# A fused Fourier transform and MLP: relayouts that read two slots twice, and a new order of the opening

## The chip, the cores and the metric

The kernel runs on one core of one Trainium2 chip. The core has a matrix engine (PE; its weight loads are PEld), a vector engine (DVE), an activation engine (ACT), a general engine (POOL), and SP, which here only issues transfers. Transfers can be issued from SP, ACT and POOL, each with a queue of its own; they share 16 DMA engines. The metric is the device time of one execution in microseconds, lower is better.

## The reference

For an input `x` of 8 batches x 3136 rows x 256 columns, what must be computed is

```python
X = np.fft.fft(x, axis=1)
X = np.fft.fft(X, axis=2)
x = X.real
mu, var = x.mean(-1), x.var(-1)
xn = (x - mu) / np.sqrt(var + 1e-06) * g_ln
out = x + np.maximum(xn @ w_ch1, 0.0) @ w_ch2
```

with `w_ch1` of 256 x 1024 and `w_ch2` of 1024 x 256. Both weights arrive as float64, and the kernel takes them apart on the chip.

## The kernel before, in words

**Two steps of the long transform.** 3136 = 64 x 49. Step 1 makes length-64 transforms: for each batch, seven pairs of slots, folded on DVE or POOL (`fold_zw`, `fold_eo`), multiplied on PE (`step1`, L272 to L280), copied from PSUM by ACT (L284), and stored by `store1` (L288) to a scratch in DRAM. The scratch holds 16 slots of 128 x 256 floats. Step 1 fills 14; the other two are cleared once for each of the two scratches by `clear_scratch` (L236), from zeros in the tile `warm`.

**The relayout.** `relayout` (L291, transfer on L295) reads the scratch back into a tile `s2` with another meaning of the 128 rows: row = slot * 8 + r, with 16 groups of 256 floats in each row. The source steps through 16 slots of 8 rows, 128 rows at one distance; each row is a run of up to 4096 floats. Batch 0 is read in four pieces (groups 0 to 2, 2 to 4, 4 to 8, 8 to 16: 256, 256, 512 and 1024 KB). Batches 1 to 7 are read in one transfer of 2048 KB each.

**Step 2 and the MLP.** `step2` (L328) multiplies `s2` by a table `tab_s`, a group at a time; it uses the first 112 rows (14 slots) as K. L332 adds the zero frequency, once a batch, in the first `step2` of that batch. ACT casts the result to `ckh` (L349) and copies it to `ck` (L351), and DVE makes the rest `ckl` (L353). Then the tokens run in chunks of 256, in 8 steps of a chunk each: `moe1_a` (L373: w1 in a high and a low part, 6 matmuls; ACT copies to `asb`, L378; DVE makes `h`, L379 and L380), `moe1_b` (ACT makes `h_hi`, L387; DVE `h_lo`, L388) and `moe2` (L423: w2 in two parts, 12 matmuls). `residual` and its helpers (L448 and on) do the row transform and the statistics, `finish` (L493 and on) the result, and `store_out` (L504) the stores of 256 KB.

**The weights.** Both float64 weights come in four quarters. `convert_z` on ACT (L550) takes the exponent, `convert_m` on DVE (L541, L543) the mantissa, `convert_b` on DVE (L555 a maximum, L556 a shift) mends the exponent, and `finish_w1` or `finish_w2` (L584, L616) multiplies. `transform_w1` (L594), `round_w1` (L602), `rest_w1` (L607) and `rest_w1_copy` (L612) fold a transform into w1; they need the tile `minus` (L775). `split_w2` makes w2's two parts on ACT (L560) and POOL (L561). The w2 quarters are loaded by `load_w2` (L575) into the tiles that held the w1 quarters, so each waits for w1's conversions from that tile.

**What sets the order.** PE, ACT, DVE and POOL run in an order written out by hand. The start is the long list of calls in the function's last part, in which SP keeps the written order too. Afterwards a loop over the steps of all chunks calls `moe1_b`, `moe1_a`, what a table `late` has for that step, `moe2` of three steps before, and what a table `after` has. Relayouts of batches 1 to 7 stand in `after`, 2 steps behind the batch's last store.

## Time and profile before

| What | Value |
|---|---|
| Median of 3 runs | 989.21 us (988.85 to 989.91) |
| The profiled execution | 989.4 us, of which the span is 987.6 us |
| PE busy | 975.3 us, 99% of the span |
| DVE, ACT, POOL busy | 813.1, 535.3, 249.8 us |
| Granted TensorE clock | 1.00 |
| Moved by DMA | 94.94 MB, 96 GB/s in the mean |
| A whole relayout, issue to landing | 7.9 us median, 7 of them |

Busy time is that in which an engine executes something. A row of the timeline gives the start and the length in us, then the engine, line and operation with its output and inputs, and in brackets the idle time before it with what ended that. "Issue to landing" of a transfer goes from the instruction that issues it to the last byte's arrival. Windows cut the span in stretches and list each engine's busy time within. A line of the waits has the engine and line that waits, what it waited for, the sum in us, how often, and the longest.

### The profile page before, as it was taken

The page shows a single profiled execution, that of the slowest core. Times are in us where ns is not written, and L with a number is a line of the kernel's source. Part 1 is how long each engine was busy: PE and PEld are TensorE (multiplying, and loading weights), DVE is VectorE, ACT ScalarE, POOL GpSimd, SP SyncE. Part 2 cuts the span into 40 slices and gives each one's busy share as a digit, 9 for nine tenths or more (in the row PEclk, how much of TensorE's full clock was granted, in tenths as well). Part 3 has the DMA queues.
Part 4 walks back from the last instruction along what each step waited for, and adds up shares of the span by engine and source line. Part 5 has one row for each costly group of instructions (what it writes and reads, how often), then busy time and mean ns, then how long its engine had stood idle before and what let it go on. Part 6 is the DMA issues. An engine that isn't in the chain of part 4 may idle for free.

```text
span 987.6 us, 22017 instructions
## 1 busy us (share of the span) xinstructions
PE 975.3 (99%) x8410; PEld 961.6 (97%) x8411; DVE 813.1 (82%) x2194; ACT 535.3 (54%) x1416; POOL 249.8 (25%) x279
## 2 busy tenths in 40 slices
PE   9899999999999999999999999999999999999998
PEld 5689999999999999999999999999999999999998
DVE  6788887888888888878888888888888888888887
ACT  3656555555555555555555556555555554555553
POOL 2147343224322332322342234223322300000000
PEclk9999999999999999999999999999999999999999
DMA  9923352214221242112421232212311112100101
GB/s 350 377 80 130 101 188 76 87 54 158 79 96 55 76 168 90 65 65 71 176 86 55 86 150 87 97 55 73 121 52 37 54 50 102 44 23 22 44 23 44
DMA packets 42297, 94.94 MB, mean 96 GB/s; under 512 B 4240, under 2 KB 19088, under 8 KB 41168
## 3 DMA queue, kind: packets, MB, share of 16 engines
q1 hardware_dynamic: 40016, 90.19, 25.4%
q10 hardware_dynamic: 1776, 2.04, 0.6%
q8 instruction: 67, 1.10, 0.5%
q0 software_dynamic: 400, 1.31, 0.3%
q14 instruction: 38, 0.31, 0.1%
HBM read 52.62 MB, written 40.89 MB: 95 GB/s over the span
## 4 chain that ended last, share of the span: by engine, by line
PE 94%; DVE 3%; DMA 1%; ACT 1%; issue 0%; ACTq 0%; SPq 0%; DVEq 0%
PE acc L423 52%; PE ab L373 26%; PE ps L328 6%; PE psy L448 5%; PE ps L280 3%; DVE h_lo L388 1%; DMA scratch<-s 1%; PE pw L701 1%; PE ps L272 0%; DMA s<-scratch 0%; PE ps L274 0%; DVE h L379 0%; DVE h L380 0%; ACT h_hi L387 0%; PE bb L373 0%
## 5 line engine op out<-in xcount | busy, mean ns | idle before, releaser
L423 PE MATMUL acc<-w_hi,h_lo 128*128 128x256 f32 x1568 | 434.1, 277 | 1.2 <-ACT w_hi L560 0.9
L423 PE MATMUL acc<-w_lo,h_hi 128*128 128x256 f32 x1568 | 433.8, 277 | 1.0 <-POOL w_lo L561 1.0
L423 PE MATMUL acc<-w_hi,h_hi 128*128 128x256 f32 x1568 | 433.6, 277 | 0.0
L388 DVE SCALAR_TENSOR_TENSOR h_lo<-h,h_hi 128x512 fp32r<-128x512 f32 x392 | 294.7, 752 | 141.8 <-ACT h_hi L387 139.3
L387 ACT ACTIVATE h_hi<-h 128x512 fp32r<-128x512 f32 x392 | 250.1, 638 | 292.2 <-DVE h L380 292.1
L423 PEld LDWEIGHTS acc<-w_hi,h_lo 128*128 128x128 f32 x1568 | 294.6, 188 | 1.9 <-ACT w_hi L560 1.1
L423 PEld LDWEIGHTS acc<-w_lo,h_hi 128*128 128x128 f32 x1568 | 294.4, 188 | 1.2 <-POOL w_lo L561 1.2
L423 PEld LDWEIGHTS acc<-w_hi,h_hi 128*128 128x128 f32 x1568 | 294.5, 188 | 0.0
L373 PE MATMUL ab<-ckl,w_hi 128*128 128x256 f32 x768 | 218.1, 284 | 2.2 <-DVE h L380 2.1
L373 PE MATMUL ab<-ckh,w_lo 128*128 128x256 f32 x768 | 212.8, 277 | 0.3 <-ACT ckh L349 0.3
L373 PE MATMUL ab<-ckh,w_hi 128*128 128x256 f32 x768 | 212.5, 277 | 0.0
L231 POOL TENSOR_TENSOR fl<-f,fh 128x512 fp32r<-128x512 f32 x49 | 64.0, 1306 | 504.6 <-ACT fh L225 472.5
L379 DVE TENSOR_TENSOR h<-asb,ab 128x256 f32<-128x256 f32 x384 | 158.6, 413 | 1.3 <-ACT asb L378 1.3
L380 DVE TENSOR_TENSOR h<-asb,ab 128x256 f32<-128x256 f32 x384 | 158.7, 413 | 0.0
L373 PEld LDWEIGHTS ab<-ckl,w_hi 128*128 128x128 f32 x768 | 144.3, 188 | 3.4 <-issue 3.4
L373 PEld LDWEIGHTS ab<-ckh,w_lo 128*128 128x128 f32 x768 | 144.4, 188 | 0.5 <-ACT ckh L349 0.5
L373 PEld LDWEIGHTS ab<-ckh,w_hi 128*128 128x128 f32 x768 | 144.3, 188 | 0.0
L378 ACT COPY asb<-ab 128x256 f32<-128x256 f32 x384 | 137.8, 359 | 8.9 <-PE ab L373 1.3
L284 ACT COPY s<-ps 128x508 f32<-128x508 f32 x56 | 32.8, 585 | 62.6 <-PE ps L280 51.2
L328 PE MATMUL ps<-tab_s,s 112*128 112x98 f32 (+1 forms) x512 | 65.6, 273 | 1.0 <-DMA s<-scratch 1.0
L328 PEld LDWEIGHTS ps<-tab_s,s 112*128 112x128 f32 x512 | 61.8, 192 | 1.5 <-issue 1.5
L349 ACT CAST ckh<-ps 128x392 fp32r<-128x392 f32 (+49 forms) x112 | 39.7, 356 | 41.8 <-PE ps L328 41.5
(113 smaller groups left out, 969.1 us busy)
## 6 DMA issues: line engine op xcount, KB each, us to landing
xs<-x SPq DMA_DIRECT2D x56, 512.0 KB, 4.4
out<-o SPq DMA_DIRECT2D x96, 256.0 KB, 2.0
s<-scratch SPq DMA_DIRECT2D x7, 2048.0 KB, 7.9
scratch<-s SPq DMA_DIRECT2D x49, 256.0 KB, 2.4
w1p_all<-w SPq DMA_DIRECT2D x6, 512.0 KB, 8.9
scratch<-s POOLq DMA_DIRECT2D x4, 256.0 KB, 6.6
w1p_all<-w ACTq DMA_DIRECT2D x2, 512.0 KB, 5.6
s<-scratch SPq DMA_DIRECT2D x1, 1024.0 KB, 10.8
```

Of the source, the lines that this page charges most:

```text
L231: nc.gpsimd.tensor_tensor(out=lo, in0=f, in1=hi.bitcast(F32), op=ALU.subtract)
L284: nc.scalar.copy(s[:, :, :, :127], ps[:, :, :, :127])
L328: nc.tensor.matmul(ps[:, h, k0 - base:k1 - base], s2[b][:KP, g, 128 * h:128 * h + 128], tab_s[:KP, h, k0:k1], start=(h == 0 and g == 2 * j ...
L349: nc.scalar.copy(hi, src)
L373: nc.tensor.matmul(pt, wt[wi][:, j, fs], ch[xi][:, j, :w], start=(n == 0), stop=(n == 2))
L378: nc.scalar.copy(asb[:, :w], pa)
L379: nc.vector.tensor_tensor(out=h[:, :w], in0=asb[:, :w], in1=pb, op=ALU.add)
L380: nc.vector.tensor_tensor(out=h[:, w:], in0=asb[:, :m], in1=pb[:, :m], op=ALU.subtract)
L387: nc.scalar.activation(h_hi, h, AF.Relu)
L388: nc.vector.scalar_tensor_tensor(out=h_lo, in0=h, scalar=0.0, in1=h_hi.bitcast(F32), op0=ALU.max, op1=ALU.subtract)
L423: nc.tensor.matmul(acc[c, i][:, side], hs[xi][:, h0:h0 + 128], ws[wi][:, f], start=(f == 0 and side == 0 and n == 0), stop=(f == 7 and n = ...
L448: nc.tensor.matmul(ps[:, j, :n], ck[:, j], ty_s[:, j, :n], start=(j == 0), stop=True, skip_group_check=True)
```

## The change

Five things change.

1. The scratch has 14 slots, and nothing is cleared. A relayout reads 16 slots all the same: eight from slot 0 on and eight from slot 6 on, so slots 6 and 7 are read twice. The source of the transfer is written as 2 groups at a distance of 6 slots, 8 slots in each, and the rows of a slot; the 8 slots and their 8 rows are at one distance and make 64 rows. The destination stays 128 rows. The second copy of slots 6 and 7 falls on rows 64 to 79 of `s2`. The table has zeros there, and `step2` multiplies over all 128 rows.
2. The first piece of `tab` is issued by ACT, behind the last store of batch 0 and the load of w2's first quarter, and no longer by SP ahead of them. The first quarter of w2 is loaded ahead of ACT's conversion of w1's third quarter; the second quarter is loaded by SP between two pieces of the relayout, and no longer by ACT; the third comes behind the third piece.
3. The maximum (`convert_x`, from `convert_b`) moves from DVE to POOL for w1's last two quarters and all four of w2.
4. Conversions, splits and copies of the opening stand at other places: w2's second quarter ahead of the first cast to `ckh`, the split of `t1` near it, the copies to `ck` later, w2's last quarter earlier.
5. The first chunk's second `residual_e` comes one step later.

**SP around the relayout of batch 0.** `s_0` is the tile `s2`, `w1p_all` the tile in which the quarters of w2 arrive. Before:

```order
L570 DMA w1p_all<-w 128x512 x2
L760 DMA tab_s<-tab 128x2x393
L761 DMA tz_s<-tz 128x50
L295 DMA s_0_259<-scratch_93 128x512 x2
L575 DMA w1p_all<-w 128x2x256
L295 DMA s_0_259<-scratch_93 128x1024
L773 DMA tab_s<-tab 128x2x392
L295 DMA s_0_259<-scratch_93 128x2048
L575 DMA w1p_all<-w 128x2x256
```

Changed:

```order
L574 DMA w1p_all<-w 128x512 x2
L763 DMA tz_s<-tz 128x50
L292 DMA s_0_262<-scratch_93 128x1x512 x2
L579 DMA w1p_all<-w 128x2x256
L292 DMA s_0_262<-scratch_93 128x1x1024
L579 DMA w1p_all<-w 128x2x256
L777 DMA tab_s<-tab 128x2x392
L292 DMA s_0_262<-scratch_93 128x1x2048
L579 DMA w1p_all<-w 128x2x256
```

The piece of `tab` ahead of `tz` is gone, a load of w2 stands between the two small pieces and the third, another behind the third, and the destination of a relayout has a dimension of 1 in it.

**ACT behind the last store of batch 0.** `ew_2` and `ew_3` are exponents of w1's last two quarters. Before:

```order
L288 DMA scratch_93<-s_0_134 128x2x256
L550 ACTIVATE ew_2_245<-w1p_all 128x512
L575 DMA w1p_all<-w 128x2x256
L550 ACTIVATE ew_3_252<-w1p_all 128x512
L575 DMA w1p_all<-w 128x2x256
L775 CAST minus<-tw_all 128x128
```

Changed:

```order
L283 DMA scratch_93<-s_0_134 128x2x256
L579 DMA w1p_all<-w 128x2x256
L550 ACTIVATE ew_2_244<-w1p_all 128x512
L550 ACTIVATE ew_3_251<-w1p_all 128x512
L768 DMA tab_s<-tab 128x2x393
L779 CAST minus<-tw_all 128x128
```

ACT issues one load of w2 in place of two, ahead of both conversions, then the piece of `tab`, and `minus` stands behind that.

**ACT around the first casts of step 2.** `ps_0` and `ps_1` are step 2's results, `ew_1` the exponent of w2's second quarter, `fw_0` its first quarter. Before:

```order
L602 CAST w_hi<-psw_296 128x512
L560 CAST w_hi<-fw_0_309 128x512
L349 CAST ckh_327<-ps_0_320 128x2x195
L349 CAST ckh_327<-ps_1_331 128x2x61
L550 ACTIVATE ew_1_341<-w1p_all 128x512
L378 COPY asb_361<-ab_354 128x256
```

Changed:

```order
L606 CAST w_hi<-psw_294 128x512
L564 CAST t_hi<-tu_s 128x128
L550 ACTIVATE ew_1_315<-w1p_all 128x512
L345 CAST ckh_332<-ps_0_325 128x2x195
L345 CAST ckh_332<-ps_1_336 128x2x61
L374 COPY asb_355<-ab_348 128x256
```

The second quarter's conversion stands ahead of the two casts to `ckh`, where it was behind them, and the first quarter's split has gone to a later place.

**ACT around w2's last quarter** (`ew_3` from `w1p_all`). Before:

```order
L349 CAST ckh_480<-ps_2_474 128x2x75
L351 COPY ck_479<-ps_2_474 128x2x75
L387 ACTIVATE h_hi_519<-h_496 128x512
L378 COPY asb_530<-ab_523 128x256
L550 ACTIVATE ew_3_535<-w1p_all 128x512
L387 ACTIVATE h_hi_559<-h_531 128x512
L378 COPY asb_570<-ab_563 128x256
```

Changed:

```order
L347 COPY ck_479<-ps_2_474 128x2x75
L550 ACTIVATE ew_3_518<-w1p_all 128x512
L383 ACTIVATE h_hi_526<-h_494 128x512
L374 COPY asb_537<-ab_530 128x256
L383 ACTIVATE h_hi_562<-h_538 128x512
```

The conversion comes one `h_hi` and one `asb` earlier.

The diff:

```diff
--- before.py
+++ after.py
@@ -100,7 +100,7 @@
                         rows[:, 0, t:t + n], rows[:, 1, t:t + n] = ((c, s), (-s, c))[comp]
             t += n
     tab = tab.transpose(3, 0, 1, 2, 4, 5).reshape(KP, 2, HALF)
-    tab = np.concatenate([tab, np.zeros((128 - KP, 2, HALF))])
+    tab = np.concatenate([tab[:64], np.zeros((128 - KP, 2, HALF)), tab[64:]])
     tz = np.concatenate([tz.reshape(4 * NS, 50), np.zeros((128 - 4 * NS, 50))])
     d = np.arange(1, 129)[:, None]
     ang = 2 * np.pi * ((d * np.arange(129)) % D) / D
@@ -185,7 +185,7 @@
 
     e0c, s1, scratch, s2, zw, pieces = {}, {}, {}, {}, {}, {}
     for b in range(2):
-        scratch[b] = dram.tile([16, 128, D], F32, tag=f"scratch{b}", name=f"scratch{b}", bufs=1)
+        scratch[b] = dram.tile([NS, 128, D], F32, tag=f"scratch{b}", name=f"scratch{b}", bufs=1)
 
     def ends(b, p0=0, p1=NS, eng=nc.gpsimd):
 
@@ -230,11 +230,6 @@
         lo = moving.tile([128, 2, 2, 128], F32R, tag="f_lo", name=f"fl{b}_{i}", bufs=2)
         nc.gpsimd.tensor_tensor(out=lo, in0=f, in1=hi.bitcast(F32), op=ALU.subtract)
         pieces[b, i] = (hi, lo)
-
-    def clear_scratch(b, eng):
-
-        in_order(eng.dma_start(scratch[b][NS:].rearrange("s p d -> p s d"),
-                               warm.rearrange("p (s d) -> p s d", s=2)))
 
     def alloc1(b):
         if b not in s1:
@@ -291,9 +286,10 @@
     def relayout(b, g0=0, g1=16, eng=nc.sync):
         if b not in s2:
             s2[b] = weights.tile([128, 16, D], F32, tag="s2", name=f"s2_{b}", bufs=2)
-        sv = scratch[b].rearrange("s (r g) d -> s r (g d)", g=16)
-        in_order(eng.dma_start(s2[b][:, g0:g1].rearrange("r g d -> r (g d)"),
-                               sv[:, :, g0 * D:g1 * D]))
+        sv = scratch[b].rearrange("s (r g) d -> s r (g d)", g=16)[:, :, g0 * D:g1 * D]
+        slot, *inner = [list(a) for a in sv.ap]
+        sv = bass.AP(sv.tensor, sv.offset, [[(NS - 8) * slot[0], 2], [slot[0], 8], *inner])
+        in_order(eng.dma_start(s2[b][:, g0:g1].rearrange("r g d -> r (g d)"), sv))
 
     gb = group_bounds()
     chunk = {}
@@ -325,8 +321,8 @@
         for g in (2 * j, 2 * j + 1) if "m" in part else ():
             k0, k1 = gb[g], gb[g + 1]
             for h in range(2):
-                nc.tensor.matmul(ps[:, h, k0 - base:k1 - base], s2[b][:KP, g, 128 * h:128 * h + 128],
-                                 tab_s[:KP, h, k0:k1], start=(h == 0 and g == 2 * j), stop=True,
+                nc.tensor.matmul(ps[:, h, k0 - base:k1 - base], s2[b][:, g, 128 * h:128 * h + 128],
+                                 tab_s[:, h, k0:k1], start=(h == 0 and g == 2 * j), stop=True,
                                  skip_group_check=True)
             if g == 0:
                 nc.tensor.matmul(ps[:, 1, 0:50], zmu[:, b % 2], tz_s[:KP], start=False, stop=True,
@@ -544,15 +540,23 @@
                                        op0=ALU.mult, op1=ALU.add)
         conv[key] = wp, e, f
 
+    def convert_zx(key, wp):
+        convert_z(key, wp)
+        convert_x(key)
+
     def convert_z(key, wp):
         _, e = conv[key][:2] if key in conv else convert_e(key, wp)
         top = wp.bitcast(BF16).rearrange("p (n four) -> p n four", four=4)[:, :, 3]
         nc.scalar.activation(e, top, AF.Prelu, scale=2.0 ** -112, alpha=2.0 ** 32)
 
-    def convert_b(key):
-        _, e, f = conv[key]
-        i, u = e.bitcast(I16), e.bitcast(U16)
-        nc.vector.tensor_scalar(out=i, in0=i, scalar1=-28672, scalar2=None, op0=ALU.max)
+    def convert_x(key, eng=nc.gpsimd):
+        i = conv[key][1].bitcast(I16)
+        eng.tensor_scalar(out=i, in0=i, scalar1=-28672, scalar2=None, op0=ALU.max)
+
+    def convert_b(key, both=True):
+        if both:
+            convert_x(key, nc.vector)
+        u = conv[key][1].bitcast(U16)
         nc.vector.tensor_scalar(out=u, in0=u, scalar1=3, scalar2=0xFF80,
                                 op0=ALU.logical_shift_left, op1=ALU.bitwise_and)
 
@@ -679,7 +683,7 @@
         add_late(8 * c + 10 + (c < 2), inverse_std, c)
         for i in range(2):
             add(s, residual, c, i)
-            add_late(s + 1, residual_e, c, i)
+            add_late(s + 1 + (c == 0 and i), residual_e, c, i)
             add_late(s + i + 2, residual_y, c, i)
             add_late(8 * c + 11 + i, finish, c, i)
             add(8 * c + 11 + i, store_out, c, i)
@@ -741,7 +745,6 @@
             step1_ends(0, 6, 10)
             store1(0, 3, nc.scalar)
             store1(0, 4, nc.gpsimd)
-            clear_scratch(0, nc.gpsimd)
             for i in (5, 6):
                 fold_zw(0, i, nc.vector)
                 fold_eo(0, i, nc.vector)
@@ -757,87 +760,90 @@
             finish_w1(1)
             step1(0, 6)
             store1(0, 6, nc.scalar)
-            nc.sync.dma_start(tab_s[:, :, :gb[4]], tab[:, :, :gb[4]])
             nc.sync.dma_start(tz_s, tz)
-            convert_z("w1_2", w1p[2])
             load_w2(0, nc.scalar)
+            convert_zx("w1_2", w1p[2])
             convert_m("w1_2", w1p[2])
-            convert_z("w1_3", w1p[3])
-            load_w2(1, nc.scalar)
-            convert_b("w1_2")
+            convert_zx("w1_3", w1p[3])
+            nc.scalar.dma_start(tab_s[:, :, :gb[4]], tab[:, :, :gb[4]])
+            convert_m("w1_3", w1p[3])
+            convert_b("w1_2", False)
             finish_w1(2)
             relayout(0, 0, 2)
             relayout(0, 2, 4)
+            load_w2(1)
+            relayout(0, 4, 8)
             load_w2(2)
-            relayout(0, 4, 8)
             nc.sync.dma_start(tab_s[:, :, gb[4]:gb[8]], tab[:, :, gb[4]:gb[8]])
             relayout(0, 8, 16)
             nc.scalar.copy(minus, tw_all[:, 512:])
             transform_w1(0, 0)
             transform_w1(0, 1)
             round_w1(0)
-            convert_m("w1_3", w1p[3])
-            convert_b("w1_3")
+            convert_b("w1_3", False)
             load_w2(3)
             nc.sync.dma_start(ty_s, ty)
             nc.sync.dma_start(tab_s[:, :, gb[8]:], tab[:, :, gb[8]:])
             for i in range(NU):
                 load_x(1, i)
-            clear_scratch(1, nc.sync)
             finish_w1(3)
             transform_w1(1, 0)
             rest_w1(0)
-            convert_z("w2_0", w2p[0])
+            convert_zx("w2_0", w2p[0])
             rest_w1_copy(0)
             transform_w1(1, 1)
             round_w1(1)
             convert_m("w2_0", w2p[0])
-            convert_b("w2_0")
-            split_w2(0, finish_w2(0))
+            convert_b("w2_0", False)
+            f0 = finish_w2(0)
+            split(t1_hi, t1_lo, tu_s[:, 0:128])
+            convert_zx("w2_1", w2p[1])
+            convert_m("w2_1", w2p[1])
             warm_up(2, warm_h)
             step2(0, "m")
-            step2(0, "hl")
+            step2(0, "h")
+            step2(0, "l")
             step2(1, "m")
-            step2(1, "hl", 0)
-            convert_m("w2_1", w2p[1])
-            convert_z("w2_1", w2p[1])
-            convert_b("w2_1")
-            convert_m("w2_2", w2p[2])
+            step2(1, "h", 0)
+            step2(1, "l", 0)
+            convert_b("w2_1", False)
+            f = finish_w2(1)
             moe1_a(0, ((1, 0), (0, 0), (0, 1)))
+            split_w2(0, f0)
             moe1_a(1, ((1, 0), (0, 0), (0, 1)))
             rest_w1(1)
             moe1_b(0)
+            split_w2(1, f)
+            moe1_a(2)
+            moe1_b(1)
+            moe1_a(3)
+            moe1_b(2)
+            rest_w1_copy(1)
+            convert_zx("w2_2", w2p[2])
+            convert_m("w2_2", w2p[2])
             step2(0, "f")
-            rest_w1_copy(1)
-            moe1_a(2)
-            f = finish_w2(1)
-            moe1_b(1)
-            split_w2(1, f)
-            moe1_b(2)
-            moe1_a(3)
             step2(1, "f")
-            convert_z("w2_2", w2p[2])
             step2(1, "hl", 1)
             moe2(0)
             moe1_b(3)
+            moe2(1)
             moe1_a(4)
-            convert_b("w2_2")
+            convert_b("w2_2", False)
             f = finish_w2(2)
             nc.gpsimd.tensor_scalar(out=neg, in0=ty_s[:, 1, 129:130], scalar1=2.0, scalar2=-1.0,
                                     op0=ALU.mult, op1=ALU.add)
-            moe2(1)
             step2(2, "m")
             moe1_b(4)
+            moe1_a(5)
             split_w2(2, f)
-            moe1_a(5)
             step2(2, "hf")
             step2(2, "l")
             moe2(2)
-            add_late(6, convert_a, "w2_3", w2p[3])
-            add_late(7, convert_b, "w2_3")
-            add_late(7, lambda: w2f.append(finish_w2(3)))
-            add_late(7, lambda: split_w2(3, w2f.pop()))
-            add_late(14, split, t1_hi, t1_lo, tu_s[:, 0:128])
+            convert_zx("w2_3", w2p[3])
+            convert_m("w2_3", w2p[3])
+            add_late(6, convert_b, "w2_3", False)
+            add_late(6, lambda: w2f.append(finish_w2(3)))
+            late[7].insert(0, (lambda: split_w2(3, w2f.pop()), ()))
 
         main.append(True)
         lag, last = 3, 8 * NCH
```

## The prediction

> **What bounds the kernel now.** I read the page first (span, busy time, chain), then the table of windows for the opening against the rest, then the opening's timeline, and last the relayouts from issue to first use.
>
> The page and the windows (length, busy time of PE, weight loads, DVE, ACT, POOL, granted clock, DMA share, GB/s):
>
> ```profile
> span 987.6 us, 22017 instructions
> PE 975.3 (99%) x8410; PEld 961.6 (97%) x8411; DVE 813.1 (82%) x2194; ACT 535.3 (54%) x1416; POOL 249.8 (25%) x279
> PE 94%; DVE 3%; DMA 1%; ACT 1%; issue 0%; ACTq 0%; SPq 0%; DVEq 0%
> ...
> 20.00:30.00 10.00, 8.09 (x18) 2.90 (x18) 7.84 (x17) 5.39 (x12) 0.00 (x0) 1.00 0.98 352
> 30.00:40.00 10.00, 7.36 (x56) 6.75 (x56) 6.09 (x16) 5.28 (x13) 1.25 (x1) 1.00 0.99 380
> 40.00:50.00 10.00, 9.56 (x79) 9.10 (x78) 8.46 (x19) 6.98 (x19) 3.17 (x3) 1.00 1.01 402
> 50.00:60.00 10.00, 8.15 (x68) 7.60 (x66) 8.54 (x21) 4.46 (x12) 4.49 (x6) 1.00 0.06 19
> 200.00:400.00 200.00, 200.00 (x1769) 200.00 (x1768) 167.94 (x451) 110.95 (x295) 62.02 (x68) 1.00 0.27 97
> ```
>
> PE sets the time. From 200 to 400 us it has no idle moment. All that a better order can win lies in the opening: 1.91 us idle in the window from 20, 2.64 in that from 30, 0.44 and 1.85 in the next two. The 16 DMA engines are full (0.98 to 1.01) until well past 40 us, so in the opening a transfer lands when the bytes ahead of it have gone.
>
> The opening, from the chain, the timeline and the waits:
>
> ```profile
> 20.06 5.82 DMA scratch<-s
> 26.10 4.49 DMA s<-scratch
> ...
> 30.72 0.66 PE L328 MATMUL ps<-tab_s,s 112*128 112x99 f32 x4 [1.05 <-DMA s<-scratch]
> 32.09 0.48 ACT L349 CAST ckh<-ps 128x390 fp32r<-128x390 f32 x1 [1.71 <-PE ps L328]
> 37.09 0.36 PE L373 MATMUL ab<-ckl,w_hi 128*128 128x256 f32 x1 [1.57 <-DVE h L380]
> 49.75 0.67 ACT L550 ACTIVATE ew<-w1p_all 128x512 bf16<-128x512 bf16 x1
> ...
> ACT minus L775 <- DMA scratch<-s: 4.0, 1, 4.0
> ```
>
> The last store of batch 0 lands at 25.88, the first piece of its relayout at 30.59, and step 2 starts at 30.72. ACT stands 4.0 us ahead of `minus`, behind the issue of a w2 load. The conversion of w2's last quarter starts at 49.75.
>
> **The change, part by part.** The relayout is the part that repeats: once in pieces, then seven times whole. How it stands now, and how much room each whole one has until its first use (L332 marks the first step 2 of a batch):
>
> ```profile
> DMA packets 84, 1.38 MB, mean 393 GB/s; under 512 B 0, under 2 KB 0, under 8 KB 0
> q1 hardware_dynamic: 84, 1.38, 95.2%
> ...
> s<-scratch SPq DMA_DIRECT2D x7, 2048.0 KB, 7.9
> ...
> 125.80 0.33 SPq L295 DMA_DIRECT2D s<-scratch  x1
> 233.53 0.33 SPq L295 DMA_DIRECT2D s<-scratch  x1
> 352.42 0.33 SPq L295 DMA_DIRECT2D s<-scratch  x1
> 467.88 0.33 SPq L295 DMA_DIRECT2D s<-scratch  x1
> 581.19 0.33 SPq L295 DMA_DIRECT2D s<-scratch  x1
> 697.29 0.33 SPq L295 DMA_DIRECT2D s<-scratch  x1
> 813.54 0.33 SPq L295 DMA_DIRECT2D s<-scratch  x1
> ...
> 148.43 0.35 PE L332 MATMUL ps<-tz_s,zmu 112*128 112x50 f32 x2
> 264.62 0.35 PE L332 MATMUL ps<-tz_s,zmu 112*128 112x50 f32 x2
> 380.79 0.35 PE L332 MATMUL ps<-tz_s,zmu 112*128 112x50 f32 x2
> 496.98 0.35 PE L332 MATMUL ps<-tz_s,zmu 112*128 112x50 f32 x2
> 613.15 0.34 PE L332 MATMUL ps<-tz_s,zmu 112*128 112x50 f32 x2
> 729.34 0.35 PE L332 MATMUL ps<-tz_s,zmu 112*128 112x50 f32 x2
> 844.19 0.34 PE L332 MATMUL ps<-tz_s,zmu 112*128 112x50 f32 x2
> ```
>
> The first two lines are the DMA view from 235.5 to 239 us, inside the relayout issued at 233.53. 84 packets carry 1.38 MB, 16.4 KB each: a packet is one of the 128 rows of 4096 floats. All sixteen engines are busy for 95.2% of 3.5 us, so one engine moves 1.38 MB / (0.952 x 16 x 3.5 us) = 25.9 KB/us. The whole 2.10 MB then takes 5.06 us; of the 7.9 us to landing, 2.8 are fixed. The room from issue to first use is 22.6, 31.1, 28.4, 29.1, 32.0, 32.1 and 30.7 us, together 205.9.
>
> The bytes of a relayout stay the same. What changes is the outermost count of its source. Before, source and destination both step through 128 rows. Now the source steps through 2 groups of slots, then 64 rows. If a transfer is dealt to the engines by shares of its outermost count, two groups fill two engines. Every transfer that the kernel issues now leads with 128 rows on its chip side, so the trace shows no other count: the bounds of a relayout are 7.9 us (sixteen engines) and 1049 KB / 25.9 + 2.8 = 43.3 us (two). I take two: the packets show that rows are dealt whole, and a deal by the first count is the simplest one that gives sixteen equal shares of 128.
>
> The Trainium skill's page "DMA: Bandwidth & Descriptors", section "Why a DMA increments its semaphore by 16 and not by 1", says the same: a transfer issued by SP or ACT looks at the slowest dimension of each side that is not 1 and uses the largest number of engines up to 16 that divides both. By that rule 128 against 128 gives 16, which the 95.2% agrees with, and 2 against 128 gives 2, which no run here shows yet.
>
> With two engines each whole relayout lands 43.3 us after its issue. PE waits 43.3 less the room: 7 x 43.3 - 205.9 = **97 us**. Work in order behind that matmul on PE waits too, so nothing fills the gap.
>
> Batch 0: four pieces of together 2.10 MB, again 40.5 us on two engines. The loads that SP issues among them (w2_1, w2_2, a piece of tab, then w2_3: 1.97 MB over sixteen engines) add 123 KB to those two, 4.8 us. Started from a last store at about 24.5 us, w2_3 lands at 24.5 + 40.5 + 4.8 + 2.8 = 72.6 us, where its conversion ran at 49.75: **23 us** late. ACT converts it in its order, so the casts behind it (asb, h_hi) and then PE wait. The pieces themselves are used one by one and come earlier than that.
>
> Eight stalls of 10 to 23 us leave PE idle far longer than any gap after 8 us now. What an idle PE does is shown only at the start, where the same shape, 128x512, has two prices:
>
> ```profile
> 1.49 3.78 PE L701 MATMUL pw<-warm 128*128 128x512 f32 x4 [1.49 <-DVE warm L708]
> ...
> 23.44 1.99 PE L594 MATMUL psw<-gw,tw_all 128*128 128x512 f32 x4 [0.40 <-DVE gw L584]
> ```
>
> 0.95 us each after the idle start, 0.50 when running: four lose 1.8 us. If every stall costs that, 8 x 1.8 = 14 us; if none does, 0. No row tells which, and I take the middle, **7 us**.
>
> The Trainium skill, page "TensorE: Matmul & The Clock Gate", section "Part 1: The HAM clock gate", states that about 3.4 us of idling halve the clock and about as long a busy stretch restores it. By it the eight restarts would lose an estimated 8 x 1.7 = 14 us, the upper of the two bounds; that an idle stretch within the kernel does it, no run here shows.
>
> The other edits move things of the opening. Two clears (0.26 MB each) and their two DMAs go, one from POOL's queue, one from SP's. One clear and the first piece of tab (0.40 MB) no longer run ahead of the last store; at 16 x 25.9 = 414 KB/us that is 1.6 us, so the store would land at 24.3. The piece of tab follows w2_0 on ACT instead, 1.0 us more in a full pipe, and is there before the relayout's first piece, which waits for the store. ACT no longer stands behind w2_1's issue; w2_1 goes to SP between the second and the third piece and holds the third back by 1.3 us, which nothing waits for so early. Matrices of 128 rows for 112 add nothing on PE by count: as many matmuls stream as many columns. The maxima go from DVE to POOL, six of them:
>
> ```profile
> L826 POOL TENSOR_SCALAR neg<-ty_s 128x1 f32<-128x1 f32 x1 | 0.6, 621 | 0.0
> L561 POOL TENSOR_TENSOR w_lo<-fw,w_hi 128x512 fp32r<-128x512 f32 x4 | 5.1, 1272 | 32.1 <-ACT w_hi L560 32.1
> L555 DVE TENSOR_SCALAR ew<-ew 128x512 int16<-128x512 int16 x8 | 2.4, 297 | 0.3 <-ACT ew L550 0.3
> ...
> L388 DVE SCALAR_TENSOR_TENSOR h_lo<-h,h_hi 128x512 fp32r<-128x512 f32 x392 | 294.7, 752 | 141.8 <-ACT h_hi L387 139.3
> ...
> 41.90 1.35 DVE L388 SCALAR_TENSOR_TENSOR h_lo<-h,h_hi 128x512 fp32r<-128x512 f32 x1 [0.62 <-ACT h_hi L387]
> ```
>
> A maximum costs 0.30 us on DVE. On POOL it lies between 0.62 (one element a row) and 1.27 (512 floats, two inputs), nearer the second: 0.3 to 1.0 us longer in the chain of a quarter, and it frees DVE by 0.3. While POOL subtracts, DVE's h_lo took 1.35 us, against 0.75 in the page's mean, so POOL's use is not free. With two engines this is covered by the stall of batch 0. Without that cover it is the second rival.
>
> **The sum**, against the profiled execution: 987.6 + 97 + 23 + 7 = 1114.6 us of span. That execution took 989.4, 1.8 outside the span, and is 0.2 over the median of 989.21. So **1116 us**. The engines' pace gives its own range; the DMA view from 12 to 17 us has, in forty slices,
>
> ```profile
> GB/s 393 328 459 459 459 393 328 459 459 459 393 328 459 459 459 426 295 459 459 426 393 360 459 426 459 348 373 389 414 389 389 451 418 422 463 369 393 459 360 459
> ```
>
> At 28.7 KB/us (459 over sixteen, the level that many slices reach) a relayout takes 39.3 us, the stalls come to 69, the opening to 18, a cold start to nothing: 1077. At 25.1 (402 from 40 to 50 us, full engines) it is 44.6, 106, 24 and 14: 1133. So 1077 to 1133.
>
> **The rivals.**
>
> (1) The transfer is spread on all sixteen engines, and the opening gains. For it: rows of 16 KB are equal packets, and these could be dealt singly. Against it: the trace has no example of another count. The store lands at 24.3 and the first piece 4.5 later, at 28.8. Then the cast at 32.09 waits for w2_1: behind the second piece (0.6) the 0.52 MB take 1.3, and the conversion 0.67: about 31.5, a gain of 0.6. The 1.57 us at 37.09 go, since w2_1 and w2_2 are no longer converted between the first h's, and the 1.85 of the window from 50, since the last quarter is converted earlier. 987.6 - 4.0 + 1.8 = **985.4 us**, not slower. It decides if more than some eight engines are used: at eight a relayout needs 10.1 + 2.8 us, inside every room.
>
> (2) Sixteen engines, but the gain is eaten. Four maxima of w2 at up to 1.0 us more each are 4 us in the opening's chains; w2_1 now stands before ckh, so each microsecond that it lands later goes straight to PE. 985.4 + 3.6 = **989 us**. For it: DMA stays full until past 40 us. Against it: POOL has 4.49 busy in the window from 50, and is idle from 20 to 30.
>
> (3) Two engines, but the w2 loads aren't held behind them (each engine could take from several queues in turn). Then the 23 us shrink to the pieces' own lateness, some 5 to 10: **1100 us**, inside the forecast's own range.
>
> **How the numbers follow.** Two engines with its variant (3): 0.68, of which the variant has 0.13. Rival (1): 0.24. Rival (2): 0.08, of which about a sixth still is faster. A difference under 0.2%, 2 us, can't be told from none. Faster then is 0.25, the same 0.07, slower 0.68. The predicted time is the likeliest case's, 1116. Since the sixteen-engine cases hold more than 2 in 10, the range reaches down to them: 982 to 1134; the case's own is given above.
>
> **What would show it.** Right: the seven whole relayouts land 39 to 45 us after their issue; the DMA view over one of them shows a share of about 2/16; PE's first step 2 of each batch waits for s<-scratch for 9 to 23 us, seven times; ACT's conversion of w2_3 starts past 65 us; the first matmuls after each stall take nearly double. Wrong: landings stay near 8 us, step 2 has no wait for s<-scratch after batch 0, and the change's whole effect lies before 62 us. If the landing is long but PE's waits are shorter than 43 less the room, relayouts are issued earlier than the order shows, or engines run faster alone than sixteen together.

## The result, and the profile after

The changed kernel takes 1148.1 us (median of 5, 1143.8 to 1150.5) against 989.7 us; the ratio is 1.160, with a 95% interval of 1.158 to 1.162. The forecast was 1116 us, with 1134 as the upper end: the direction and the mechanism were right, the size was 32 us short. The profiled execution took 1150.5 us, with a span of 1148.7.

The page of the changed kernel (span, busy time, shares of the chain that ended last):

```profile
span 1148.7 us, 22012 instructions
PE 1011.4 (88%) x8411; PEld 996.7 (87%) x8411; DVE 813.6 (71%) x2188; ACT 536.8 (47%) x1416; POOL 255.8 (22%) x284
PE 61%; DMA 34%; DVE 3%; ACT 1%; POOL 0%; issue 0%; SPq 0%; ACTq 0%
```

The chain was 94% PE and 1% DMA before; now a third of it is DMA. The span grew by 161.1 us in two parts. PE's idle time (span less busy) went from 12.3 to 137.3 us, 125 more. PE's busy time went from 975.3 to 1011.4, 36 more, with as many matmuls.

The idle time lies where step 2 begins. The timeline of the changed kernel, the first and last issue of a whole relayout, and PE's first step 2 of each batch from 1 to 7:

```profile
155.88 0.54 SPq L292 DMA_DIRECT2D s<-scratch  x1
955.49 0.51 SPq L292 DMA_DIRECT2D s<-scratch  x1
...
200.16 1.18 PE L324 MATMUL ps<-tab_s,s 128*128 128x99 f32 x4 [19.58 <-DMA s<-scratch]
333.27 1.17 PE L324 MATMUL ps<-tab_s,s 128*128 128x99 f32 x4 [13.96 <-DMA s<-scratch]
469.34 1.17 PE L324 MATMUL ps<-tab_s,s 128*128 128x99 f32 x4 [16.29 <-DMA s<-scratch]
604.42 1.18 PE L324 MATMUL ps<-tab_s,s 128*128 128x99 f32 x4 [15.70 <-DMA s<-scratch]
735.75 1.17 PE L324 MATMUL ps<-tab_s,s 128*128 128x99 f32 x4 [12.89 <-DMA s<-scratch]
865.18 1.17 PE L324 MATMUL ps<-tab_s,s 128*128 128x99 f32 x4 [10.15 <-DMA s<-scratch]
997.86 1.17 PE L324 MATMUL ps<-tab_s,s 128*128 128x99 f32 x4 [10.82 <-DMA s<-scratch]
```

Seven stalls, 99.4 us together. From issue to first use the first relayout took 200.16 - 155.88 = 44.3 us, the last 42.4. The DMA view from 181 to 188 us, while the first relayout runs alone:

```profile
DMA packets 23, 0.38 MB, mean 54 GB/s; under 512 B 0, under 2 KB 0, under 8 KB 0
q1 hardware_dynamic: 23, 0.38, 12.6%
```

12.6% of sixteen engines is two engines. A packet takes 0.126 x 16 x 7 us / 23 = 0.61 us, the pace of before (0.952 x 16 x 3.5 / 84 = 0.63).

The other part is the clock. Windows behind the first stall (length, busy time with instructions of PE, weight loads, DVE, ACT, POOL, then the granted clock, DMA share, GB/s):

```profile
202.00:204.00 2.00, 2.00 (x11) 2.00 (x11) 0.92 (x3) 0.94 (x3) 0.00 (x0) 0.50 0.42 167
204.00:206.00 2.00, 2.00 (x12) 2.00 (x12) 0.09 (x1) 1.52 (x5) 0.00 (x0) 0.56 0.12 40
206.00:208.00 2.00, 2.00 (x19) 2.00 (x19) 1.41 (x4) 1.15 (x6) 0.00 (x0) 1.00 0.00 0
```

Back at work, PE ran at half clock until about 205.8 us: 11 or 12 matmuls in 2 us, then 19. Set against PE's gaps, the clock's records give 57.8 us in which PE worked at half clock, so 28.9 lost: 40.2 us behind the seven stalls, 17.6 in the opening, where the records of the kernel before, which begin at 7.7 us, have none.

A smaller part of the busy time lies behind the last two stalls. Two windows of the changed kernel, ahead of the sixth stall and behind it:

```profile
760.00:800.00 40.00, 40.00 (x355) 40.00 (x354) 32.59 (x88) 22.69 (x62) 9.96 (x10) 1.00 0.18 67
900.00:940.00 40.00, 40.00 (x344) 40.00 (x343) 32.47 (x90) 21.36 (x56) 9.95 (x10) 1.00 0.11 41
```

The granted clock is 1.00 in both, yet 344 matmuls run where 355 did. The matmuls of `moe2` start 117.8 ns after one another there, 113.3 elsewhere.

The opening of the changed kernel, PE's waits in the timeline and ACT's in the table of waits (sum, times, longest):

```profile
24.91 3.64 PE L598 MATMUL psw<-gw,tw_all 128*128 128x512 f32 x4 [2.42 <-DVE gw L588]
37.96 2.03 PE L324 MATMUL ps<-tab_s,s 128*128 128x98 f32 x8 [3.99 <-DMA s<-scratch]
78.97 2.09 PE L444 MATMUL psy<-ty_s,ck 128*128 128x129 f32 x8 [19.83 <-DMA ty_s<-ty]
...
ACT ew L550 <- DMA w1p_all<-w: 35.2, 6, 21.2
```

Loads behind the pieces of the relayout come late, w2's quarters on ACT, and on PE the small table `ty` that SP issues behind w2's last quarter.

### The profile page after: what moved, and what is told of

Read it like the earlier page. It is cut to its first block, busy times and chain, and to the rows that moved or that the text cites. A ratio compares the mean times of both kernels' runs of the same rounds, so it can differ in the third digit from the quotient of the medians.

```text
span 1148.7 us, 22012 instructions
## 1 busy us (share of the span) xinstructions
PE 1011.4 (88%) x8411; PEld 996.7 (87%) x8411; DVE 813.6 (71%) x2188; ACT 536.8 (47%) x1416; POOL 255.8 (22%) x284
## 4 chain that ended last, share of the span: by engine, by line
PE 61%; DMA 34%; DVE 3%; ACT 1%; POOL 0%; issue 0%; SPq 0%; ACTq 0%
PE acc L419 33%; DMA s<-scratch 27%; PE ab L369 17%; PE ps L324 5%; PE psy L444 4%; DMA ty_s<-ty 3%; PE ps L275 3%; DMA w1p_all<-w 2%; DMA scratch<-s 1%; DVE h_lo L384 1%; DMA xs<-x 1%; DVE h L375 0%; DVE h L376 0%; ACT h_hi L383 0%; ACT s L279 0%; DMA tu_s<-tu 0%
## 5 line engine op out<-in xcount | busy, mean ns | idle before, releaser
L369 PE MATMUL ab<-ckl,w_hi 128*128 128x256 f32 x768 | 222.1, 289 | 1.6 <-DVE h L376 1.4
L369 PE MATMUL ab<-ckh,w_lo 128*128 128x256 f32 x768 | 216.4, 282 | 0.4 <-ACT ckh L345 0.4
L369 PE MATMUL ab<-ckh,w_hi 128*128 128x256 f32 x768 | 216.0, 281 | 0.0
L324 PE MATMUL ps<-tab_s,s 128*128 128x98 f32 (+1 forms) x512 | 76.0, 298 | 107.3 <-DMA s<-scratch 103.4
L324 PEld LDWEIGHTS ps<-tab_s,s 128*128 128x128 f32 x512 | 70.2, 213 | 109.4 <-DMA s<-scratch 104.9
L369 PEld LDWEIGHTS ab<-ckl,w_hi 128*128 128x128 f32 x768 | 147.8, 192 | 2.5 <-issue 2.3
L369 PEld LDWEIGHTS ab<-ckh,w_hi 128*128 128x128 f32 x768 | 147.5, 192 | 0.0
L493 DVE SCALAR_TENSOR_TENSOR o<-acc,r,y 128x256 f32<-128x256 f32 x96 | 45.9, 478 | 116.6 <-DMA out<-o 116.5
L444 PE MATMUL psy<-ty_s,ck 128*128 128x130 f32 (+1 forms) x396 | 61.0, 302 | 19.8 <-DMA ty_s<-ty 19.8
```

The source lines that it names most:

```text
L324: nc.tensor.matmul(ps[:, h, k0 - base:k1 - base], s2[b][:, g, 128 * h:128 * h + 128], tab_s[:, h, k0:k1], start=(h == 0 and g == 2 * j), s ...
L369: nc.tensor.matmul(pt, wt[wi][:, j, fs], ch[xi][:, j, :w], start=(n == 0), stop=(n == 2))
L444: nc.tensor.matmul(ps[:, j, :n], ck[:, j], ty_s[:, j, :n], start=(j == 0), stop=True, skip_group_check=True)
L493: nc.vector.scalar_tensor_tensor(out=o[:, 1], in0=ps[:, 1], scalar=r, in1=y[:, D:0:-1], op0=ALU.mult, op1=ALU.add)
```

## The experiments

### Which part of the change costs the time

**Sixteen engines, two slots still read twice.** The relayout is issued in two halves of 64 rows:

```diff
-        sv = bass.AP(..., [[(NS - 8) * slot[0], 2], [slot[0], 8], *inner])
-        in_order(eng.dma_start(s2[b][:, g0:g1]..., sv))
+        for h in range(2):
+            in_order(eng.dma_start(s2[b][64 * h:64 * h + 64, g0:g1]...,
+                                   sv[(NS - 8) * h:(NS - 8) * h + 8]))
```

> The changed kernel with each relayout written as two transfers of 64 rows (slots 0 to 7, slots 6 to 13): same bytes, slots 6 and 7 still read twice, nothing cleared, same order of engines. Theory (the engines of a transfer are shares of its outermost count): 64 rows are dealt to all sixteen, a whole relayout lands 8 to 9 us after its issue, no stall of PE at a batch's start, granted clock 1.00, and 984 to 988 us. Rival A (reading two slots twice, or the missing clears, make it slow): near 1148 us. Rival B (the new order makes it slow): above 1050 us.

Measured: 988.2 us, ratio 0.998 (0.997 to 0.999). The stalls are gone, so reading twice is not what is slow. Rival A falls, and so does B. But the landing is slower than the 8 to 9 us expected: from the first issue to the end of the last packet, the two halves together take 11.5 to 13.4 us, the whole relayout before 7.3 to 8.6. The page (each half alone), and the DMA view from 577.3 to 581.9 us:

```profile
s<-scratch SPq DMA_DIRECT2D x14, 1024.0 KB, 10.2
...
DMA packets 55, 0.90 MB, mean 196 GB/s; under 512 B 0, under 2 KB 0, under 8 KB 0
q1 hardware_dynamic: 55, 0.90, 89.5%
```

All engines are busy, and a packet takes 0.895 x 16 x 4.6 / 55 = 1.20 us, double. This is taken up below.

**The new order alone.** Scratch of 16 slots, clears, table and relayout as before, all the rest as changed:

```diff
-        scratch[b] = dram.tile([NS, 128, D], ...)
+        scratch[b] = dram.tile([16, 128, D], ...)
+            clear_scratch(0, nc.gpsimd)
-        sv = bass.AP(..., [[(NS - 8) * slot[0], 2], [slot[0], 8], *inner])
+        sv = scratch[b].rearrange("s (r g) d -> s r (g d)", g=16)
```

> The changed kernel with the relayout of before (16 slots, two of them cleared, 128 rows at one distance, table and matmuls as before); the new order, the moved loads and the maximum on POOL stay. Theory: 985 to 990 us, landing of a whole relayout near 8 us; what it differs from the split kernel is what the clears cost in the opening, 0 to 2 us. Rival A: as before, 989. Rival B (the new order makes it slow): above 1050 us.

Measured: 984.5 us, ratio 0.995 (0.993 to 0.997). Its page and windows:

```profile
s<-scratch SPq DMA_DIRECT2D x7, 2048.0 KB, 7.9
...
30.00:40.00 10.00, 8.77 (x68) 7.86 (x67) 8.14 (x20) 7.18 (x18) 4.55 (x4) 1.00 1.03 391
50.00:60.00 10.00, 9.65 (x81) 9.26 (x80) 8.40 (x26) 4.94 (x15) 7.11 (x9) 1.00 0.18 63
```

PE works 8.77 us of the window from 30, 7.36 before, and 9.65 of that from 50, 8.15 before: the gain is in the opening, where the first rival had it. Step 2 of batch 1 starts at 143.0 us, 148.0 before, and from there on both kernels take the same. Its 985.4 us was 0.9 off.

**The new relayout alone,** in the old order:

> The kernel before with the new relayout alone (two groups of slots in one transfer, 14 slots, no clears, zeros in rows 64 to 79 of the table); the old order, the maximum on DVE. Theory: whole relayouts land 42 to 45 us after their issue, PE stalls seven times for 10 to 20 us (some 99 us together), half clock after each, and 1130 to 1155 us. Rival B (the new order is to blame): 985 to 995 us.

```diff
-        sv = scratch[b].rearrange("s (r g) d -> s r (g d)", g=16)
+        sv = bass.AP(..., [[(NS - 8) * slot[0], 2], [slot[0], 8], *inner])
```

Measured: 1154.4 us, ratio 1.167 (1.164 to 1.169), 6 us more than with the new order. The page and the first stall:

```profile
PE 1013.3 (88%) x8410; PEld 998.0 (87%) x8411; DVE 813.8 (71%) x2194; ACT 535.4 (46%) x1416; POOL 245.3 (21%) x278
...
201.39 0.96 PE L324 MATMUL ps<-tab_s,s 128*128 128x99 f32 x3 [20.98 <-DMA s<-scratch]
```

The loss is the relayout's, all of it; the order gains 5 to 6 us with either relayout.

### How the engines are chosen, and what else sets their pace

**Four groups.** The 16 slots lie in four groups with an unused slot between, nothing is read twice:

```diff
+        sv = bass.AP(..., [[5 * slot[0], 4], [slot[0], 4], *inner])
```

> As the new order with the old relayout, but the 16 slots lie in four groups of 4 in the scratch, with one unused slot between groups, so that the source steps through 4 groups of 32 rows; nothing is read twice. Theory: four engines, 524 KB each at 25.9 KB/us, landing 20.2 + 2.8 = 23 us after the issue; that is within or 0.5 us over the room of 22.6 to 32 us, so no stall of a batch over 2 us; the opening ends 5 to 15 us later than with sixteen engines; 990 to 1005 us. Rival A (only reading twice is slow): 8 us to landing, as the new order with the old relayout. Rival C (any such source goes to two engines): near 1148 us.

Measured: 1085.7 us, ratio 1.097 (1.090 to 1.105). That was a miss of all three expectations: far from 1000, and not 1148. The timeline, and the DMA view from 167 to 173 us:

```profile
141.34 0.56 SPq L297 DMA_DIRECT2D s<-scratch  x1
...
179.23 1.18 PE L329 MATMUL ps<-tab_s,s 112*128 112x99 f32 x4 [13.18 <-DMA s<-scratch]
...
DMA packets 26, 0.43 MB, mean 71 GB/s; under 512 B 0, under 2 KB 0, under 8 KB 0
q1 hardware_dynamic: 26, 0.43, 25.4%
```

25.4% is four of sixteen engines: the count went as expected. But a packet takes 0.254 x 16 x 6 / 26 = 0.94 us, and the relayout 37.9. Something beside the count of engines sets the pace. If each engine gets one group, two engines write rows 64 apart in the changed kernel, and here four write rows 32 apart.

**Eight groups** of 2 slots, 16 rows to an engine:

```diff
-        sv = bass.AP(..., [[5 * slot[0], 4], [slot[0], 4], *inner])
+        sv = bass.AP(..., [[3 * slot[0], 8], [slot[0], 2], *inner])
```

> As the kernel with four groups, but eight groups of 2 slots with an unused slot between: the source steps through 8 groups of 16 rows, eight engines. The four groups took 37 to 40 us to land where 23 were expected, with packets of 0.61 us and of 1.22 us side by side. Theory C (only the count of engines sets the pace): 262 KB on each engine, 10.1 + 2.8 = 13 us to landing. Theory P (two engines that write rows 32 apart in the destination share one way in, each then at half pace; with 16 rows to an engine, engines n and n+2 meet): packets of about 1.25 us, 18 to 23 us to landing. Both within the room of the batches, so at most 1 us of stall each; 985 to 995 us.

Measured: 997.8 us, ratio 1.008 (1.006 to 1.010). The DMA view from 605 to 610 us:

```profile
DMA packets 35, 0.57 MB, mean 115 GB/s; under 512 B 0, under 2 KB 0, under 8 KB 0
q1 hardware_dynamic: 35, 0.57, 50.1%
```

Eight engines, and 0.501 x 16 x 5 / 35 = 1.15 us a packet. The last of the 16 KB packets ends 20 to 24 us after the issue, theory P. No batch stalls; the loss is in the opening, and puts the time 3 us over the 985 to 995 expected.

**Two engines, rows 32 apart, and rows 16 apart.** The two kernels differ in how many transfers a relayout is cut into, each with a leading count of two:

```diff
+        for q in range(2):     # rows 32 apart; 4 transfers of [[3 * slot, 2], [slot, 2]] for 16 apart
+            src = bass.AP(..., sv.offset + q * 10 * slot[0], [[5 * slot[0], 2], [slot[0], 4], *inner])
+            in_order(eng.dma_start(s2[b][64 * q:64 * q + 64, g0:g1]..., src))
```

> As the kernel with four groups, but in two transfers of 2 groups of 32 rows each, so two engines, whose destination rows lie 32 apart (0 to 31 and 32 to 63, then 64 to 95 and 96 to 127). Same bytes for each engine as in the changed kernel, where the two engines' rows lie 64 apart. Theory P (rows 32 apart share a way in): packets of 0.9 to 1.25 us on two engines, 60 to 80 us to landing, 1290 to 1450 us. Theory C (only the count of engines): packets of 0.61 us, 44 us to landing, 1140 to 1160 us.

> Its control: four transfers of 2 groups of 16 rows each, again two engines, whose destination rows lie 16 apart. Theory P and theory C alike: packets of 0.61 us, 43 to 46 us to landing, 1140 to 1165 us. If its packets take 0.9 us and more too, what slows the one of 32 rows is the smaller pieces, not where the rows lie.

Measured, one execution each: 1264.2 us with rows 32 apart and 1134.1 us with rows 16 apart. The kernel with rows 32 apart, its first stall and the DMA view from 176 to 189 us:

```profile
223.36 0.96 PE L331 MATMUL ps<-tab_s,s 112*128 112x99 f32 x3 [41.12 <-DMA s<-scratch]
...
DMA packets 25, 0.41 MB, mean 32 GB/s; under 512 B 0, under 2 KB 0, under 8 KB 0
q1 hardware_dynamic: 25, 0.41, 13.0%
```

The kernel with rows 16 apart, from 179 to 188 us:

```profile
DMA packets 29, 0.48 MB, mean 53 GB/s; under 512 B 0, under 2 KB 0, under 8 KB 0
q1 hardware_dynamic: 29, 0.48, 12.4%
```

Two engines in both. A packet takes 1.08 us where the rows are 32 apart, 0.62 where they are 16 apart. The bytes, the count of engines and the leading count are the same. Both times are lower than expected, 1264 by 26 us and 1134 by 6. With rows 32 apart a third of the packets took 0.6 us all the same, as if the pair drifted out of step at times.

These windows are short. The mean over all 896 packets of the seven whole relayouts is 0.65 us in the changed kernel, 0.66 with two engines 16 rows apart and 0.93 with two 32 apart; it is 1.07 with four groups, 1.23 with eight and with the two halves, and 0.72 in the kernel before. So the number of engines that the leading counts allow limits the pace, and, as far as these runs go, engines at work together whose rows lie 32 apart slow each other.

Two things keep the second from being shown in full. The two engines with rows 32 apart also read slots 5 apart, where those with rows 16 apart read slots 3 apart. With eight groups the engines whose rows lie 32 apart read slots 6 apart, as the two of the changed kernel do, and were slow all the same, which speaks for the rows. And no trace names the rows that an engine gets. If each engine got an even share of neighbouring rows, the halves of 64 rows would have such pairs, but so would the plain relayout of 128 rows, which is fast. Either its rows are dealt in another way, or the distance of the rows is not the whole cause; no run here tells which.

The Trainium skill's page "SBUF — State Buffer", section "Door 1: The DMA port swizzle", maps partitions n and n + 32 to the same port of 16, and n + 64 to another one. The packets agree: 0.61 us with 64 apart, 1.08 with 32 apart. The rule on the count of engines (the Trainium skill, "DMA: Bandwidth & Descriptors", section "Why a DMA increments its semaphore by 16 and not by 1") is borne out too: leads of 2, 4 and 8 against 128 gave shares of 12.6, 25.4 and 50.1%.

**112 rows.** Fourteen slots to 112 rows, nothing read twice and nothing cleared:

```diff
+        in_order(eng.dma_start(s2[b][:KP, g0:g1].rearrange("r g d -> r (g d)"), sv))
```

> The new order with a relayout of the 14 slots alone, 112 rows to 112 rows, nothing read twice, nothing cleared, table and matmuls over 112 rows as in the kernel before. Theory: 112 is a multiple of 16, so sixteen engines of 7 rows: 1.84 MB, 4.4 + 2.8 = 7.2 us to landing if no two engines meet, up to 11.7 if they meet in pairs all the time; no stalls; 983 to 988 us. Rival (only 128 rows are dealt to all): landing over 20 us and over 1000 us.

Measured: 985.0 us, ratio 0.996 (0.994 to 0.997). The page:

```profile
s<-scratch SPq DMA_DIRECT2D x7, 1792.0 KB, 10.0
```

Less is moved in more time, 10.0 us against 7.9, and a packet takes 0.99 us in the mean, as it would if engines of seven rows met part of the time (that they do is not shown); within the room of the batches that costs nothing. It does what the change set out to do (no clears) and is not told apart from the 984.5 us with the clears: what the clears cost, and what the slower rows cost in the opening, are either nothing or cancel.

### The clock, and the loads behind the relayout

**PE kept at work.** Matmuls of zeros ahead of the first step 2 of each batch, in number to fill the stall but for a microsecond:

```diff
+        if j == 0 and b and "m" in part:
+            for i in range((86, 60, 70, 68, 55, 42, 45)[b - 1]):
+                nc.tensor.matmul(ps..., warm_h[:, :128], warm_h, start=True, stop=True)
```

> The changed kernel, with 42 to 86 matmuls of zeros ahead of each batch's first step 2, which fill all but about 1 us of the seven stalls as they were measured; they change no result. Theory (after an idle stretch PE runs at half clock for some 5 to 6 us and loses about 3): granted clock 1.00 at the seven restarts, PE's busy time without the fillers down by 20 to 28 us, 1120 to 1130 us. Rival (the time beyond the idle stretches lies elsewhere: ACT, DVE or the stores): still 1143 to 1152 us.

Measured: 1139.2 us (1137.2 to 1145.6), ratio 1.153 (1.149 to 1.156); against the changed kernel's 1148.1 that is 9 us less, and 13 between the profiled executions. The expectation, 1120 to 1130 us and 20 to 28 less busy time, was missed. The timeline and a window behind the first stall:

```profile
180.10 18.51 PE L323 MATMUL ps<-warm_h 128*128 128x512 bf16 x84
199.19 0.69 PE L328 MATMUL ps<-tab_s,s 128*128 128x99 f32 x4 [0.58 <-DMA s<-scratch]
...
200.00:204.00 4.00, 4.00 (x37) 4.00 (x37) 2.92 (x8) 3.23 (x12) 0.00 (x0) 1.00 0.28 109
```

Here the clock stayed at 1.00, and 37 matmuls ran in 4 us. The work of batch 1, from its first step 2 to the next batch's stall, took 116.5 us; it was 119.2 in the changed kernel and 116.35 before. But in three of the seven places the clock still fell for one or two spells of 3.4 us, where shorter gaps were left, so 8 of the 20 us stayed lost. In all, PE worked at half clock for 35.0 us, 57.8 in the changed kernel, so the clock is 11.4 of the 13. The work behind the sixth stall took 115.1 us, 121.9 in the changed kernel, where it had the slower matmuls; why they did not come here is open. The clock is shown to be the cause of most of what a restart costs where it was kept; a remainder of 0.1 to 1.4 us a restart (the four where it was kept) is not the clock, and was not looked into.

**Two loads on another queue.** w2's last quarter and `ty` are issued by ACT, and so are not in SP's queue behind the relayout:

```diff
-            load_w2(3)
-            nc.sync.dma_start(ty_s, ty)
+            load_w2(3, nc.scalar)
+            nc.scalar.dma_start(ty_s, ty)
```

> The changed kernel with the load of w2's last quarter and that of ty issued by ACT instead of SP. Theory G (an engine takes the packets in order whatever queue they are in): PE still stands some 20 us ahead of its first residual matmul, 1143 to 1152 us. Theory F (each engine takes from several queues in turn, and only SP's own are held behind the relayout): both land by 50 us, the stall of 19.8 us goes, 1122 to 1135 us.

Measured: 1144.2 us, ratio 1.156 (1.152 to 1.159). The time is that of theory G, but the profile is not. PE's one long wait in the opening, and POOL's in the table of waits:

```profile
98.10 0.55 PE L369 MATMUL ab<-ckl,w_hi 128*128 128x256 f32 x1 [17.01 <-DVE h L376]
...
POOL e0c L196 <- DMA xs<-x: 24.6, 1, 24.6
```

The wait for `ty` at 59 us is gone, so loads on another queue do get past. What follows in SP's own queue, the input of batch 1, became the next to be late: POOL waits for it, ACT for POOL, and PE stands 17.0 us some 20 us later. A stall moved, and the time hardly changed (4 us less).

**The maximum** on POOL or on DVE, in the new order with the old relayout:

```diff
-            convert_zx("w2_0", w2p[0])
+            convert_z("w2_0", w2p[0])
-            convert_b("w2_0", False)
+            convert_b("w2_0")
```

and so for the other five.

> The new order with the relayout of before, and the six maxima back on DVE, at the place of the shift that follows them. Theory of the second rival (the maximum on POOL gives back what the order gains): 1 to 3 us faster than with POOL, 982 to 984 us. Theory of the first rival (POOL is idle there, and DVE is relieved): 0 to 1.5 us slower than with POOL, 984.5 to 986 us.

> The new order with the relayout of before and the maxima on POOL once more, beside the one with the maxima on DVE: 984.5 us as before; the difference to it is the maximum's.

Measured on one chip, five rounds each: 985.0 us on DVE (ratio 0.995, 0.994 to 0.997) and 985.4 on POOL (0.996, 0.994 to 0.997). No difference can be told. A maximum took 1.60 us on POOL in the mean, more than the 0.62 to 1.27 that the prediction allowed it, and 0.3 on DVE; the time does not show it.

## Why the prediction was right and wrong

- **Two engines: right.** The share was 12.6% and the pace of a packet unchanged, as in the step on the relayout. The 43.3 us to landing were 42 to 45 to first use, and the 97 us of stalls were 99.4. The room was read to L332, which runs 0.42 us behind the first matmul of step 2 (148.43 and 148.01 for batch 1), so 2.9 us were missing from the 97. That "a deal by the first count" was chosen over dealing rows singly decided the direction.
- **The opening: its idle time nearly right in size, its mechanism in part.** By the end of the work ahead of batch 1 the changed kernel was 32.4 us behind (180.6 against 148.2). PE's idle time up to there grew by 25.6 (34.3 against 8.7), where the step had 23. PE's busy time grew by 6.8, less than the 8.8 lost at half clock, in part because the records show the full clock from 4.4 us on, and from 7.7 in the kernel before. The step named the conversion of w2's last quarter alone; PE's last wait was for `ty`, which SP issues just behind that quarter, and a pause of 3.99 us for the third piece came on top.
- **The cold restarts: the step that failed.** "I take the middle, 7 us" was worth 28.9 by the clock's records, and PE's busy time grew by 36. Even the upper bound of 14 was too small, for two reasons. The price of 1.8 came from the first four matmuls of the program alone, and a restart here goes on at half clock for 4 to 7 us, 2.9 us lost on average. And stretches at half clock came eleven times, not eight: four in the opening, two of which began in gaps that are small by themselves (2.4 us at 22.5 and again at 49.8).
- **A term that was not in the sum.** The work behind the seven stalls, each up to the next one or the end, grew by 28.1 us in all over the same work before (119.2 against 116.35 us in batch 1), 20 of it clock. Of the other 8, 3.8 and 3.6 lie behind the last two stalls, where the matmuls came more slowly at a granted clock of 1.00; the cause of that stays open.
- **The sum.** The span grew by 161.1 us where the prediction had 127 (97, 23 and 7). Of the 34 that it lacks, 22 are the clock, 8 the slower work, 2.4 the stalls and 2.6 the idle time of the opening; these come to one more than the 34. The upper end of the case's own range, 1133, was built from the engines' pace and a restart of 1.8; the pace was as taken, the restart was not.
- **Rival (1)** happened as soon as the relayout was spread: 984.5 and 985.0 us against its 985.4. **Rival (2)** falls: the maximum on POOL makes no difference, though it was dearer there than priced. **Rival (3)** was right that another queue gets past and wrong about what it is worth: the next load in SP's queue takes the stall's place. Eight engines as the point from which it decides held for the batches, though only because the room was larger than what the landing took (20 to 24 us, not 12.9).

## What to carry to other kernels

Before a transfer's address pattern is rewritten, look at the outermost count on both sides: a clever first dimension of 2 can leave 14 of 16 engines idle, and a share of the DMA view near k/16 shows it at once. Price a new stall with its restart at a slower clock, here about 3 us each, and with every load queued behind the slow transfer. To get rid of padding, leave its rows out of the transfer and keep the pattern plain; the 112 rows here went to all the engines, and the time was as good as with the clears, not better.

## What the runs showed that was not expected

- Two engines whose rows lie 32 apart took 0.93 us a packet of 16 KB in the mean, against 0.66 with rows 16 apart; a relayout in two halves of 64 rows, over all the engines, took 11.5 to 13.4 us where the plain one took 7.3 to 8.6.
- The granted clock changes in spells of a multiple of 3.4 us (20.5 from 185.3 to 205.8 us in the changed kernel), and gaps shorter than a spell can bring one on, shorter also than the 3.4 us that the prediction quotes. Over all the runs here, gaps of 2.25 to 2.52 us were followed by a spell in nine cases of twelve. In the kernel with two halves a gap of 2.52 us at 22.5 was, with a spell at 24.9; in the new order with the old relayout and the maxima on POOL, one of 2.46 us at 23.0 was not. So the length of the gap alone does not decide, and what else does is open.
- The version that beats both kernels is the new order with a plain relayout: 984.5 us with the clears, or 985.0 us with 112 rows and without them, 0.5% under the kernel before.
